# A Fourier filter and an MLP mixer on one core: the first batch's filter loop, rewritten around one product per frequency

## The chip, the cores and the metric

The kernel runs on one core of one Trainium2 chip. The metric is device time in microseconds (us) of that core. The engines are TensorE (PE; its weight loads, PEld, overlap its matmuls), VectorE (DVE), ScalarE (ACT), GpSimd (POOL) and SyncE (SP). SP, ACT and POOL also issue DMAs, each from its own queue in program order. All times of single instructions come from one profiled execution.

## The reference

```python
X = np.fft.rfft(x, axis=1)                        # x: (8, 3008, 256) float32
Y = X * (filt_r + 1j * filt_i)[None]              # filt: (1505, 256)
x = np.fft.irfft(Y, n=3008, axis=1)               # float32
h = np.maximum(x.transpose(0, 2, 1) @ w_tok1, 0.0) @ w_tok2    # (3008, 256), (256, 3008)
u = x + h.transpose(0, 2, 1)
return u + np.maximum(u @ w_ch1, 0.0) @ w_ch2     # (256, 1536), (1536, 256)
```

The four mixer weights arrive as 64-bit floats. Matmuls are float32.

## The kernel before, in words

**The filter.** A length of 3008 is 47 x 64. For each batch, `a_unit` (24 of them; one matmul, `L434`, on a tile of x, then an ACT copy) makes the transform over the 64. For each of the 32 remaining frequencies k, `b_unit(k)` makes the transform over the 47 (matmul `L494` into a PSUM bank), and DVE multiplies by the filter: `p1` is the bank times the real part (`L506`), `p2` the bank's other half times the imaginary part, once with a minus sign (`L507`) and once without (`L508`). Then `bi_unit(k)` multiplies by the inverse table (`L518`). For the first batch it takes p1 and p2 as two accumulating matmuls on the same table; for later groups of two batches DVE adds them first (`L510`). ACT copies the result out (`L524`) and stores it to the scratch tensor g (`L529`), two frequencies a store. Batches go in groups: (0), (1, 2), (3, 4), (5, 6), (7).

**The loads of the loop.** The filter comes in 16 chunks of two frequencies, six DMAs each, into three buffers: chunks 1 and 2 of the first batch on SP, the others on POOL (`filt_load`, `L218` to `L225`). The real part fills the lower 64 partitions, the imaginary part the upper; `filt_double` copies the real part to the upper half on ACT (`L230`). The tables `wb` come on SP (`L454`).

**The weights.** A 64-bit weight tile is loaded to a staging buffer and converted: an ACT copy makes `top` (`L250`); DVE shifts and merges the sign (`L252`, `L253`), masks (`L255`) and computes `rest` (`L257`); top + rest is the float32 value. Twelve W1 tiles and the first `BY_PE` W2 tiles are summed on PE, by two matmuls each (`L289`, `L290`) and an ACT copy (`L292`), the other W2 tiles and the channel weights on DVE (`L278`). There are 12 W1 and 16 W2 tiles, then 2 and 10 of the channel weights. `convert()` ends one tile, starts the ACT copy of the next and issues a load some tiles ahead (`fill`).

**The opening.** Twelve tiles are converted beside the 32 frequencies of the first batch. Then the last parts of g are read back (`t4_load`, `L564`, on SP), the other 16 tiles are converted, and after 18 of the 28 tiles `token_sums(0)` is put into PE's order (96 matmul instructions, `L570`). A Relu on ACT gives h1; `u_unit` (`L600`, `L592`) needs h1 and all of W2 and makes the first 512 columns of u; then the mixer begins.

**The mixer.** For each batch there are 6 blocks of 512 (the last 448) tokens and 6 items in each (jp = 0 to 5). An item has three places. In place 0 come `up_first` (PE `L693`, DVE `up_middle`), one pending DVE step, `h_sums` of the item before (DVE, into t) and `down` part 0 of it (PE `L727`); in place 1 `up_last` (PE `L709`, then DVE and a Relu on ACT, `L714`) and, where due, a step of the next group's filter (an `a_unit`, or `b_unit(k)` with `bi_unit(k-1)`); in place 2 `down` part 1. Parts of the next block's u are made at the places (jp, place) of a map: `u_quarter` has four, with PE matmuls `L614` (and `L592` in parts 2 and 3) into a bank that DVE reads. After the last part the sums `v_steps` (t13, then t2 and t4 together, called t24) are pending DVE steps. All DVE sums have the one line `L671`.

**The banks.** The transforms, `u_quarter` and the token sums share the PSUM banks acc and b:

```python
def free_bank():
    turn.reverse()
    if turn[0] in held:
        turn.reverse()
    return turn[0]
```

`b_unit` of the later groups puts its bank into `held` until `bi_unit` reuses it. Everything is in a hand-written order (`tc.manual_schedule`); an engine runs its instructions in that order and waits for buffers.

Of the kernel before, what the change touches and what calls it, by code (L numbers as in the profile page):

```python
# [46 lines left out]
BY_PE = 6  # L47
# [77 lines left out]
def kernel(  # L125
# [68 lines left out]

    filts = [glob.tile([P, 2, KC, D], FP32, name="filt%d" % i) for i in range(FB)]
# [16 lines left out]
    def filt_load(c, first):  # L212
# [3 lines left out]
        q = nc.gpsimd if first and c not in (1, 2) else nc.sync  # L216
        for src, i, p0 in ((filt_r, 0, 0), (filt_i, 1, HALF)) + (() if first else ((filt_r, 0, HALF),)):
# [10 lines left out]
    def filt_double(c):  # L228
        t = filts[c % FB]
        nc.scalar.copy(out=t[HALF:P, 0], in_=t[0:HALF, 0])  # L230
# [11 lines left out]
    def halves(st, n, pair):  # L242
# [11 lines left out]
                                       op0=ALU.bitwise_and, op1=ALU.bitwise_or)  # L254
        nc.vector.tensor_scalar(out=rest_i, in0=top_i, scalar1=0xFF800000, scalar2=None, op0=ALU.bitwise_and)  # L255
# [12 lines left out]
    def rounded(st, n, parts, late):  # L268
# [6 lines left out]
        yield next(h)  # L275
        top, rest = next(h)
# [7 lines left out]
    def on_chip(stat, top, rest, n, parts):  # L284
# [9 lines left out]
        behind.append((ended[0] - 1, f))  # L294

    def w1_load(i):
# [13 lines left out]
        h = halves(st, 512, spare_pair())  # L310
        yield next(h)
        on_chip(wai_t, *next(h), 512, [(lambda v: v, w1[:, 2 * i:2 * i + 2, :].rearrange("p a t -> p (a t)"))])

    def w2_load(i):
# [15 lines left out]
        if i < BY_PE:  # L330
            h = halves(st, n + more, spare_pair())
            yield next(h)
            on_chip(ident, *next(h), n + more, parts)
        else:
            yield from rounded(st, n + more, parts, False)
# [42 lines left out]
    begin, copy, end = iter(tiles), iter(tiles), iter(tiles)  # L378
# [6 lines left out]
    def sum_up():  # L385
        while behind:
            behind.pop(0)[1]()

    def convert():

        ended[0] += 1
        while behind and behind[0][0] < ended[0] - 2:
            behind.pop(0)[1]()
        advance(end)
        advance(copy)
        fill(6)
# [46 lines left out]
    def dft(bs):  # L443
# [44 lines left out]
        def b_unit(k):  # L488
            tag = ("b", "pg")[k % 2] if first else free_bank()
# [10 lines left out]
            if first:  # L500
                p1, p2 = p1[:, 0:1], p1[:, 1:2]
                prods[k] = (p1, p2)
            else:
                p2 = p2p.tile([P, nb, D], FP32, tag="p2", name="p2")
                prods[k] = (p1,)
# [3 lines left out]
            if not first:  # L509
                nc.vector.tensor_tensor(out=p1, in0=p1, in1=p2, op=ALU.add)  # L510

        def bi_unit(k):


            ps = bank("acc" if first else held.pop(0)).rearrange("p (b d) -> p b d", b=2)[:, 0:nb, :]
            parts = prods.pop(k)
            for i, p in enumerate(parts):
                nc.tensor.matmul(ps[0:KR], wbs[k // WC][:, k % WC, P:], p, start=(i == 0), stop=(i == len(parts) - 1))  # L518
# [18 lines left out]
        if first:  # L537
            filt_double(0)
        for k in range(K2 + 1):
            if k < K2:  # L540
# [10 lines left out]
                if first and k % KC == KC - 1 and k + 1 < K2:  # L551
                    filt_double(k // KC + 1)
            if k >= 1:
                bi_unit(k - 1)
            yield
# [243 lines left out]
    def mix(next_ready):  # L799
# [11 lines left out]
        own = ({(3, 2): 0, (4, 2): 1}, {(2, 2): 0, (3, 2): 1, (4, 0): 2, (4, 2): 3})  # L811
# [69 lines left out]
    with tc.manual_schedule():  # L881
# [4 lines left out]
        rounds = 0  # L886
        second = dft(GROUPS[1])
        for i, _ in enumerate(dft(GROUPS[0])):
# [4 lines left out]
            if i < NXC:  # L893
                if i in (1, 3, 5, 7, 9):
                    start()
                if i == NXC - 1:
                    advance(copy)
                    for t, src in ((wa, wa_d), (wai, wai_d), (ident, ident_d)):
                        nc.scalar.dma_start(t, src)
            elif k >= 0:  # L900
                if (k + 1) * (A // 2) // K2 > k * (A // 2) // K2:
                    convert()
                    rounds += 1
# [3 lines left out]
                elif k == 25:  # L907
                    next(second)
# [9 lines left out]
        for i in range(rounds, A // 2 + TC * N2 // NG):  # L918
            convert()
            if i - rounds < XB:  # L920
                next(second)
            if i == A // 2 + BY_PE - 1:
                sum_up()
                acc = token_sums(0)
# [62 lines left out]
```

## Time and profile before

| | us |
|---|---|
| median of 7 runs | 2573.13 (2568.05 to 2574.78) |
| the profiled execution's own time | 2572.48 |
| its span, first to last instruction | 2570.7 |
| busy PE / DVE / ACT / POOL | 2493.2 / 1944.6 / 660.0 / 575.7 |
| first batch's loop over k (PE) | 30.2 to 108.6 |
| token sums of batch 0 (PE) | 123.2 to 144.0 |
| mixer's first matmul | 156.5 |

A row of the groups reads: line, engine, operation, output<-inputs, shapes and count, then busy us, mean ns of one, then idle us of the engine before them and what ended it. A row of the timeline reads: start, us, engine, line, operation, count, and in brackets the idle time before it and what ended it. PE busy is modelled for pipelined matmuls, so a busy PE is not always at its peak. The granted clock is the TensorE clock as a share of full speed.

### The profile page before, as it was taken

The page shows a single profiled execution, that of the slowest core. Times are in us where ns is not written, and L with a number is a line of the kernel's source. Part 1 is how long each engine was busy: PE and PEld are TensorE (multiplying, and loading weights), DVE is VectorE, ACT ScalarE, POOL GpSimd, SP SyncE. Part 2 cuts the span into 40 slices and gives each one's busy share as a digit, 9 for nine tenths or more (in the row PEclk, how much of TensorE's full clock was granted, in tenths as well). Part 3 has the DMA queues.
Part 4 walks back from the last instruction along what each step waited for, and adds up shares of the span by engine and source line. Part 5 has one row for each costly group of instructions (what it writes and reads, how often), then busy time and mean ns, then how long its engine had stood idle before and what let it go on. Part 6 is the DMA issues. An engine that isn't in the chain of part 4 may idle for free.

```text
span 2570.7 us, 32318 instructions
## 1 busy us (share of the span) xinstructions
PE 2493.2 (97%) x11204; PEld 2054.5 (80%) x11204; DVE 1944.6 (76%) x3668; ACT 660.0 (26%) x1312; POOL 575.7 (22%) x1051
## 2 busy tenths in 40 slices
PE   6989999999999999999999999999999999999998
PEld 3557666888888777898888777898888888898887
DVE  7897888577686998756776889856788587757776
ACT  3533222122221222212221222212222122212222
POOL 4553322211211121122121111221211121211222
PEclk8989999999999999999999999999999999999999
DMA  8864434233332332213332333213333222111100
GB/s 211 232 204 146 129 116 145 94 102 107 111 115 74 99 105 76 93 55 105 116 109 86 90 118 97 88 34 110 99 110 91 66 76 71 40 31 37 44 13 20
DMA packets 166932, 248.39 MB, mean 97 GB/s; under 512 B 35184, under 2 KB 112450, under 8 KB 166768
## 3 DMA queue, kind: packets, MB, share of 16 engines
q1 hardware_dynamic: 94176, 152.20, 19.4%
q0 software_dynamic: 32640, 46.51, 7.2%
q10 hardware_dynamic: 39952, 47.61, 5.8%
q8 instruction: 89, 1.46, 0.2%
q14 instruction: 75, 0.61, 0.1%
HBM read 168.96 MB, written 77.22 MB: 96 GB/s over the span
## 4 chain that ended last, share of the span: by engine, by line
PE 70%; DVE 18%; DMA 2%; issue 2%; ACT 2%; DVEq 0%; ACTq 0%; SPq 0%; POOL 0%; POOLq 0%
PE ps_po L727 24%; PE ps_pg L693 14%; PE ps_pg L709 10%; DVE t L671 4%; DVE hh L671 3%; PE ps_acc L570 3%; PE ps_b L614 2%; PE ps_b L570 2%; PE ps_acc L614 2%; DVE u L671 2%; DVE s L671 2%; PE ps_acc L592 2%; PE ps_b L592 2%; DVE p L508 1%; DVE p L507 1%
## 5 line engine op out<-in xcount | busy, mean ns | idle before, releaser
L772 POOL DMA_DIRECT2D out_dram<-r x757 | 410.4, 550 | 1777.8 <-ACT t L524 741.3
L671 DVE TENSOR_TENSOR hh<-ps_pg,s 128x512 f32<-128x512 f32 (+3 forms) x864 | 483.0, 587 | 281.9 <-ACT s L696 271.7
L714 ACT ACTIVATE hh<-hh 128x512 f32<-128x512 f32 (+1 forms) x576 | 347.9, 621 | 1178.3 <-DVE hh L671 1178.3
L727 PE MATMUL ps_po<-t,wc 128*128 128x256 f32 (+1 forms) x2304 | 537.2, 376 | 6.0 <-DVE t L671 5.0
L727 PEld LDWEIGHTS ps_po<-t,wc 128*128 128x128 f32 x2304 | 436.2, 190 | 130.8 <-issue 55.7
L693 PE MATMUL ps_pg<-v,wc 128*128 128x256 f32 (+1 forms) x1728 | 415.2, 377 | 2.5 <-DVE v L671 2.4
L727 PE MATMUL ps_po<-hh,wc 128*128 128x256 f32 (+1 forms) x1728 | 412.8, 375 | 0.2 <-ACT hh L714 0.2
L693 PEld LDWEIGHTS ps_pg<-v,wc 128*128 128x128 f32 x1728 | 328.1, 191 | 43.7 <-DVE v L671 6.4
L727 PEld LDWEIGHTS ps_po<-hh,wc 128*128 128x128 f32 x1728 | 328.7, 191 | 37.6 <-ACT hh L714 0.5
L709 PE MATMUL ps_pg<-u,wc 128*128 128x256 f32 (+1 forms) x1152 | 294.0, 378 | 4.3 <-DVE hh L671 4.0
L671 DVE TENSOR_TENSOR t<-t,hh 128x256 f32<-128x256 f32 (+1 forms) x576 | 244.8, 425 | 19.8
L709 PEld LDWEIGHTS ps_pg<-u,wc 128*128 128x128 f32 x1152 | 217.0, 190 | 40.1 <-DVE hh L671 13.5
L671 DVE TENSOR_TENSOR s<-ps_pg,hh 128x512 f32<-128x512 f32 (+1 forms) x288 | 196.1, 681 | 31.1 <-PE ps_pg L693 0.9
L671 DVE TENSOR_TENSOR t<-hh 128x512 f32<-128x512 f32 (+1 forms) x288 | 193.0, 670 | 0.6 <-ACT hh L714 0.6
L696 ACT COPY s<-ps_pg 128x256 f32<-128x256 f32 (+1 forms) x288 | 105.8, 367 | 338.7 <-PE ps_pg L693 314.9
L709 PE MATMUL ps_pg<-v,wc 128*128 128x256 f32 (+1 forms) x576 | 169.4, 376 | 0.0
L693 PE MATMUL ps_pg<-u,wc 128*128 128x256 f32 (+1 forms) x576 | 169.3, 376 | 0.0
L671 DVE TENSOR_TENSOR u<-ps_b,u 128x512 f32<-128x512 f32 (+3 forms) x111 | 63.5, 572 | 99.6 <-PE ps_b L614 81.0
L671 DVE TENSOR_TENSOR u<-ps_acc,u 128x512 f32<-128x512 f32 (+3 forms) x99 | 57.4, 580 | 95.4 <-PE ps_acc L614 79.2
L693 PEld LDWEIGHTS ps_pg<-u,wc 128*128 128x128 f32 x576 | 109.4, 190 | 22.6 <-issue 10.9
L709 PEld LDWEIGHTS ps_pg<-v,wc 128*128 128x128 f32 x576 | 109.2, 191 | 13.0
L518 PE MATMUL ps_acc<-p,wb 128*96 128x256 f32 (+1 forms) x256 | 97.5, 482 | 12.7 <-ACT t L524 6.1
(123 smaller groups left out, 2518.5 us busy)
## 6 DMA issues: line engine op xcount, KB each, us to landing
w<-w_tmp SPq DMA_DIRECT2D x35, 896.0 KB
g_tmp<-t ACTq DMA_DIRECT2D x128, 192.0 KB
out_dram<-r POOLq DMA_DIRECT2D x698, 32.0 KB, 1.8
x<-in_x_dram SPq DMA_DIRECT2D x173, 128.0 KB
z_tmp<-t ACTq DMA_DIRECT2D x84, 256.0 KB
t<-z_tmp SPq DMA_DIRECT2D x112, 192.0 KB
t<-g_tmp SPq DMA_DIRECT2D x42, 512.0 KB
wb<-wbi_t SPq DMA_DIRECT2D x80, 224.0 KB
```

The lines of the kernel that those rows point to most:

```text
L507: nc.vector.scalar_tensor_tensor(out=p2[re], in0=ps[im], scalar=-1.0, in1=fi, op0=ALU.mult, op1=ALU.mult)
L518: nc.tensor.matmul(ps[0:KR], wbs[k // WC][:, k % WC, P:], p, start=(i == 0), stop=(i == len(parts) - 1))
L570: nc.tensor.matmul(acc[:, t, :], w1[:, a, ts(t, P)], t4[b, a // TC4][:, a % TC4, :], start=(a == 0 and t == 0), stop=(a == A - 1 and t == ...
L592: nc.tensor.matmul(ps[:, ds(q * P, n)], t4[b, c][:, r, ts(dh, P)], wai[:, 0:n], start=(first and q == 0), stop=(not first and q == 3))
L614: nc.tensor.matmul(ps[:, ds(j * hw, hw)], h1[:, n, :], w2m[m % 2][:, at, 0:hw], start=(i < 2 and j == 0), stop=(j == len(todo) - 1))
L671: nc.vector.tensor_tensor(out=out, in0=in0, in1=in1, op=op)
L693: nc.tensor.matmul(ps[:, 0:hw], chan[0][:, jp, n, :], mov, start=True, stop=True)
L696: nc.scalar.copy(out=s[:, 0], in_=g[0][:, 0, 0:hw])
L709: nc.tensor.matmul(ps[:, 0:hw], chan[0][:, jp, n, :], mov, start=True, stop=True)
L714: nc.scalar.activation(out=hs, in_=hs, func=AF.Relu)
L727: nc.tensor.matmul(po[i][:, j, 0:hw], chan[1][:, jp, n, :], mov, start=(jp == 0 and first == 1), stop=(jp == JP - 1 and last == 1))
L772: q.dma_start(rows[g, e, :, ds(h * A + 4 * m, n)], blocks[ts(g, CW), h, e, 0:n])
```

## The change

For the first batch:

- One DVE operation multiplies the bank, read twice, by both filter parts. Both parts are loaded to the lower partitions and `filt_double` copies both to the upper ones. The sign and the swap of halves go into a second inverse table, `turn_i`, which two ACT operations per chunk make from the first (`table_turn`).
- `b_unit` takes both its banks from the pool pg, and `bi_unit` alternates between acc and b. The doubling and the table turn come after the output copy in ACT's order.
- Chunk 2 of the filter is loaded from POOL.

For the weights: a conversion has a middle and an end as separate half steps; 20 tiles instead of 12 are converted beside the loop; the ACT copies run two tiles ahead; loads run five ahead instead of six; 4 W2 tiles instead of 6 are summed on PE. `token_sums(0)` stands right behind the loop. The second group's first x loads come after the loop, and two of its a_units no longer come before the last W2 tiles.

For the mixer: in batches 1 to 7, parts 1 to 3 of `u_quarter` move to earlier places.

```diff
-BY_PE = 6
+BY_PE = 4
+IN_B = 20
...
-        q = nc.gpsimd if first and c not in (1, 2) else nc.sync
-        for src, i, p0 in ((filt_r, 0, 0), (filt_i, 1, HALF)) + (() if first else ((filt_r, 0, HALF),)):
+        q = nc.gpsimd if first and c != 1 else nc.sync
+        for src, i, p0 in ((filt_r, 0, 0), (filt_i, 1, 0 if first else HALF)) + (() if first else ((filt_r, 0, HALF),)):
...
-        nc.scalar.copy(out=t[HALF:P, 0], in_=t[0:HALF, 0])
+        nc.scalar.copy(out=t[HALF:P], in_=t[0:HALF])
+    turn_i = sp.tile([P, 4, WC, KR], FP32, tag="s", name="turn_i")
+    def table_turn(g, wb):
+        wi, to = wb[:, :, P:], turn_i[:, g % 4]
+        nc.scalar.copy(out=to[0:HALF], in_=wi[HALF:P])
+        nc.scalar.activation(out=to[HALF:P], in_=wi[0:HALF], func=AF.Copy, scale=-1.0)
...
     def convert():
-        ended[0] += 1
-        while behind and behind[0][0] < ended[0] - 2:
-            behind.pop(0)[1]()
+        convert_middle()
+        convert_end()
+    def convert_middle():
+        advance(middle)
+        sum_up()
+    def convert_end():
+        ended[0] += 1
         advance(end)
         advance(copy)
-        fill(6)
+        fill(5)
...
-            tag = ("b", "pg")[k % 2] if first else free_bank()
+            tag = "pg" if first else free_bank()
...
             if first:
-                p1, p2 = p1[:, 0:1], p1[:, 1:2]
-                prods[k] = (p1, p2)
+                nc.vector.tensor_tensor(out=p1, in0=ps.to_broadcast([P, 2, D]), in1=t[:, :, k % KC, :], op=ALU.mult)
+                prods[k] = (p1[:, 0:1], p1[:, 1:2])
+                return
...
-            ps = bank("acc" if first else held.pop(0)).rearrange("p (b d) -> p b d", b=2)[:, 0:nb, :]
+            ps = bank(free_bank() if first else held.pop(0)).rearrange("p (b d) -> p b d", b=2)[:, 0:nb, :]
...
-                nc.tensor.matmul(ps[0:KR], wbs[k // WC][:, k % WC, P:], p, start=(i == 0), stop=(i == len(parts) - 1))
+                wi = turn_i[:, k // WC % 4, k % WC] if i else wbs[k // WC][:, k % WC, P:]
+                nc.tensor.matmul(ps[0:KR], wi, p, start=(i == 0), stop=(i == len(parts) - 1))
...
-                if first and k % KC == KC - 1 and k + 1 < K2:
-                    filt_double(k // KC + 1)
             if k >= 1:
                 bi_unit(k - 1)
+            if first and k % KC == KC - 1 and k + 1 < K2:
+                filt_double(k // KC + 1)
+                table_turn(k // KC + 1, wbs[k // KC + 1])
...
-        own = ({(3, 2): 0, (4, 2): 1}, {(2, 2): 0, (3, 2): 1, (4, 0): 2, (4, 2): 3})
+        own = ({(3, 2): 0, (4, 2): 1}, {(2, 2): 0, (3, 0): 1, (3, 2): 2, (4, 0): 3})
...
-                if (k + 1) * (A // 2) // K2 > k * (A // 2) // K2:
-                    convert()
-                    rounds += 1
+                while half < 2 * IN_B * (k + 1) // K2:
+                    if half % 2:
+                        convert_end()
+                    else:
+                        convert_middle()
+                    half += 1
...
-                elif k == 25:
-                    next(second)
...
-        for i in range(rounds, A // 2 + TC * N2 // NG):
+        next(second)
+        acc = token_sums(0)
+        for _ in range(A // 2 + TC * N2 // NG - IN_B):
             convert()
-            if i - rounds < XB:
-                next(second)
-            if i == A // 2 + BY_PE - 1:
-                sum_up()
-                acc = token_sums(0)
```

## The prediction

> **What bounds the kernel now.** I read the page first. TensorE (PE) is at nine tenths or more in 37 of 40 slices; only the first, third and last are not.
>
> ```profile
> PE 2493.2 (97%) x11204; PEld 2054.5 (80%) x11204; DVE 1944.6 (76%) x3668; ACT 660.0 (26%) x1312; POOL 575.7 (22%) x1051
> PE   6989999999999999999999999999999999999998
> ```
>
> So there are two places to look: the opening 150 us, which the diff rewrites, and the long steady part, where any new PE wait is lost time. For the opening I asked for busy time by stage; columns are stretch, length, busy us of PE, weight load, DVE, ACT, POOL, granted clock, DMA share, GB/s.
>
> ```profile
> 38.20:41.80 3.60, 0.09 (x2) 0.00 (x1) 2.10 (x5) 0.98 (x2) 2.17 (x5) 1.00 0.28 77
> 84.00:108.60 24.60, 23.78 (x85) 14.06 (x84) 23.06 (x50) 11.73 (x25) 12.61 (x23) 1.00 0.82 237
> 108.60:118.00 9.40, 9.34 (x25) 4.19 (x24) 6.76 (x16) 5.93 (x13) 1.61 (x3) 1.00 1.03 215
> 123.20:144.00 20.80, 20.80 (x97) 18.05 (x95) 19.70 (x42) 6.24 (x11) 9.04 (x17) 1.00 0.87 251
> 144.00:148.60 4.60, 1.17 (x3) 0.30 (x2) 4.36 (x11) 1.34 (x3) 2.46 (x5) 0.99 0.66 179
> 148.60:154.70 6.10, 6.10 (x23) 4.11 (x24) 5.55 (x10) 1.17 (x2) 0.07 (x1) 0.73 0.01 3
> ```
>
> The first batch's loop over 32 frequencies runs from 30.2 to 108.6 us, 78.4 us, with DVE at 94% in its settled part. Then 16 weight tiles are left to convert; DVE does them until 148.6. PE runs the token sums (L570) from 123.2 to 144.0, and then waits for the last converted W2 tile:
>
> ```profile
> 142.80 1.24 PE L570 MATMUL ps_b<-t,w 128*128 128x256 f32 x5
> 144.73 1.13 PE L600 MATMUL ps_acc<-w,h 128*128 128x512 f32 x2 [0.69 <-ACT h L582]
> 148.60 2.08 PE L600 MATMUL ps_acc<-w,h 128*128 128x512 f32 x2 [2.75 <-DVE w L278]
> ```
>
> **The loop.** Prices are from its groups of instructions and DMA queues (30 to 112 us):
>
> ```profile
> L524 ACT COPY t<-ps_acc 96x256 f32<-96x256 f32 x32 | 11.8, 367 | 25.9 <-PE ps_acc L518 24.7
> L230 ACT COPY filt<-filt 64x512 f32<-64x512 f32 x14 | 8.6, 616 | 12.2 <-DMA filt<-in_filt_r_dram 6.4 <-DVE both L252 2.1 <-DVE p L506 1.6
> L507 DVE SCALAR_TENSOR_TENSOR p<-ps_b,filt 64x256 f32<-64x256 f32 x16 | 6.8, 426 | 2.1 <-DMA filt<-in_filt_i_dram 1.7
> L253 DVE SCALAR_TENSOR_TENSOR both<-st,both 128x512 uint32<-128x512 uint32 x12 | 8.3, 693 | 0.5
> q1 hardware_dynamic: 4437, 10.18, 50.7%
> q0 software_dynamic: 2976, 4.83, 22.4%
> q10 hardware_dynamic: 3134, 2.96, 12.2%
> ```
>
> DVE before: 32 products of 0.424 + 0.426 + 0.418 us are 40.6; 12 W1 conversions of 0.443 + 0.693 + 0.429 + 0.693 = 2.26 us are 27.1; with 0.025 us between operations 71 us. After: one product of 128x512 from PSUM, priced by the page's s<-ps_pg,hh row at 0.681 us, is 21.8; conversions are 12 of 2.26, four W2 tiles for PE at 1.82 and four summed on DVE at 1.82 + 0.83, 45.0; with gaps 70 us. The 19 us freed are spent on eight more tiles.
>
> PE: 32 x 6 instructions of 0.215 us, 12 W1 sums of 1.72 and four W2 sums of 1.26 make 67 us, against 62. ACT: the doubling copy grows from 512 to 1024 elements. The rows 96x256 (0.367) and 96x512 (0.572) give 0.8 ns an element, so 1.03 us, 15 of them; 30 table turns of 64x192 at 0.32 (the 96x256 row, 0.37, is the upper bound); 32 output copies, 20 rounding copies, 15 copies of sums and 16 DMA issues: 64 us against 41. DMA: the queues were busy 85.3% of 82 us, 70 us. Some six more W2 tiles (0.386 MB, at q0's 3.8 us per MB) add 8.8; the two x tiles that move behind the loop take 2.1 out: 77 us.
>
> So the loop keeps its DVE sum but loses its slack: four resources between 64 and 77 us instead of one at 71. For it: the 3.6 us hole at 38.2 (both PE and DVE waited for filter chunk 2, whose issue on SP stood behind a 7.3 us wait) goes, because chunk 2 is now issued from POOL, idle from 18 to 33 us. The single output bank's 6.1 us of PE waits for the L524 copy go too, but DVE was the later one there, so I give nothing. Against it: in-order engines with little slack wait on each other, and the doubling now needs both filter halves on ACT, ahead of rounding copies. I take a loop 1 us longer, bounds 5 us shorter (hole gone, early half clock shortened) and 9 longer (10% coupling loss on 77 us plus late filters).
>
> The Trainium skill, DMA: Bandwidth & Descriptors, section Issuing engines are not separate DMA queues, speaks against that gain: transfers issued from any engine share the same 16 DMA engines, and spreading them saves only issue time. By that rule alone the loop would be 3.6 us longer than I take it. The row decides: in that hole the DMA share was 0.28, so what lacked was the issue.
>
> **Behind the loop.** PE now goes straight to the token sums. They need the last chunk of g written and read back: before, the loop's last matmul ended at 108.6, its store was issued at 109.1, SP was released for the first last-part load at 115.7, and a load takes some 2 us: token sums could start at 118, not 123.2. Here PE has nothing to hide the 9.5 us (before, W1 and W2 sums did). An idle stretch costs clock: after 3.6 us idle before 148.6 the clock was 0.73 over 6.1 us, 3.4 us of half rate, 1.7 us lost. Sums: 118 + 20.8 + 1.7 = 140.5, Relu 0.7, first L600 at 141.2 with all W2 ready: DVE's eight tiles take 8 x 2.7 = 22 us, to 131. Gain 148.6 - 141.2 = 7.4, and 1.7 more because the 148.6 stretch no longer starts cold: 9.1, less the loop's 1: **8.1 us**. If the loop's queue drains sooner and g lands in 3 us, 3 more; if x loads or weights hold the read-back, 3 less.
>
> Two a_units of the second group lose their place beside the conversions and land among the mixer's: 2 x 0.86 = **1.7 us** back (a place with nothing else late; up to 4 if they wait for x, as the others at 160 to 190 us did).
>
> BY_PE 4 for 6 moves two tiles' sums from PE to DVE, 2 x 0.83 us, covered by the 10 us that DVE is done before the Relu; without that cover 1.7 us. Rounding copies two tiles ahead take the third of the three pairs of buffers (hh, hh, r); nothing else uses them before the mixer. Were one not free, a copy of 0.67 us would wait once a tile, in 20 tiles 13 us of ACT, which only the loop's slack there (78 - 64) hides. fill(5) begins a load when its buffer's last reader is done, so POOL no longer stands before it as it did at 99 to 111 us (12.9 us on L292); no filter load is left behind it there, so nothing is gained.
>
> **The steady part.** The second map of u_quarter places moves part 1 to (3, 0). There its PSUM bank is the one that the filter's next b_unit at (3, 1) takes: free_bank gives the bank not held. So b_unit's matmul waits for the two DVE reads of part 1, 1.15 us, queued behind h_sums:
>
> ```profile
> 1011.05 1.46 PE L727 MATMUL ps_po<-hh,wc 128*128 128x256 f32 x6
> 1012.34 0.68 DVE L671 TENSOR_TENSOR t<-hh 128x512 f32<-128x512 f32 x1
> 1012.35 1.03 PE L709 MATMUL ps_pg<-u,wc 128*128 128x256 f32 x4
> 1013.05 0.89 DVE L671 TENSOR_TENSOR t<-t,hh 128x256 f32<-128x256 f32 x2
> 1013.64 1.02 PE L494 MATMUL ps_acc<-t,wb 96*128 96x512 f32 x2
> 1018.15 1.15 DVE L671 TENSOR_TENSOR u<-ps_b,u 128x512 f32<-128x512 f32 x2 [0.29 <-PE ps_b L614]
> ```
>
> With part 1's 0.86 us of PE ahead of L709, L494 would be due at 1014.50; h_sums end at 1013.94, the bank is free at 1015.1: 0.6 us. I did the same for every such block: 12 have a b_unit there with k over 0, eleven at 0.3 us and this one, 3.9 us. Ten blocks without a filter step get t24 (0.85 us) ahead of h_sums at (5, 0), where t13 (0.68) stood; before, a 0.85 us step ahead of h_sums cost 0.12 us each time: 1.2. Behind L494 on PE stand bi_unit and the down matmuls, all delayed. **5.1 us** lost; bounds 0 (if other waits absorb it) and 7.
>
> **The sum.** -8.1 + 1.7 + 5.1 = -1.3. The profiled execution took 2572.48 us (span 2570.7); 2571.2, and its 0.65 us below the median of 2573.13 added: 2572. A measurement of this kernel can tell some 0.2%, 5.1 us, from no change, so the forecast is no change.
>
> **Rivals.** *Slower: the loop becomes bound by transfers.* Its DMA share was 0.82 to 1.08 outside the hole, and 77 us of transfers in 79 leaves nothing. Filter chunks then land late, ACT's doubling waits, and behind it output and rounding copies. It decides from a loop of 85.8 us on, 7.4 over before; at 88 the sum is 2580. Against: the last five W2 tiles begun are not needed in the loop.
>
> *Faster: the bank wait is absorbed and the hole's gain is whole.* Loop 4 us shorter, steady part +1: -13.1 + 1.7 + 1 = -10.4, 2563.
>
> *It doesn't do what it says:* u_units still wait for W2, because the eight late tiles wait for loads; first L600 at 148, a gain of 0.6 against 1.7 + 5.1: 2579.
>
> **Chances.** No change 0.39 (2568 to 2578 its own range); transfer-bound loop 0.20, late W2 0.10, together slower 0.30; faster 0.31. The range 2561 to 2584 leaves out about two in ten.
>
> **What would show it.** Right: 32 L506-like products of 0.68 us; DVE 66 to 70 us busy in the loop; loop end 105 to 114; token sums starting 8 to 11 us later after an idle, half clock PE; first L600 within 2 us of Relu; 12 new waits of L494 on DVE u. Wrong: filter DMA waits on ACT over 10 us, or no L494 waits at all.

## The result, and the profile after

The changed kernel took 2578.56 us (median of 14 runs, 2573.73 to 2583.99), the kernel before 2572.24 (34 runs, 2568.05 to 2577.19): a ratio of 1.0025 (95% interval 1.0018 to 1.0032). It is 6.3 us slower, past the 5.1 us that the prediction called no change, and inside its range.

The profiled execution is a long one (its own time 2581.64, span 2579.9, 9.2 over the span of before), so the account below adds up to 9.2, of which some 3 are this execution's. The lines move: `L494` is now `L514`, `L506` `L522`, `L518` `L539`, `L524` `L545`, `L529` `L550`, `L564` `L587`, `L570` `L593`, `L600` `L623`, `L614` `L637`, `L671` `L694`, `L218`/`L225` `L220`/`L227`, `L230` `L232`, the W2 load `L321` `L334`. The table turns are `L239` and `L240`.

First the page: PE's busy time and its 40 slices. The steady part is as full as before; the loss is in the first slices.

```profile
PE 2485.6 (96%) x11196; PEld 2052.5 (80%) x11196; DVE 1923.4 (75%) x3606; ACT 677.3 (26%) x1342; POOL 582.2 (23%) x1057
PE   7689999999999999999999999999999999999998
```

Busy time by stage, columns as before the change: stretch, length, busy PE, weight load, DVE, ACT, POOL, granted clock, DMA share, GB/s. The second row is the end of the loop, the next three the idle stretch behind it, then the token sums and the way to the mixer.

```profile
38.00:42.00 4.00, 3.88 (x14) 2.05 (x13) 2.75 (x5) 2.69 (x5) 1.70 (x4) 1.00 1.04 238
100.00:113.00 13.00, 8.27 (x32) 4.95 (x32) 11.83 (x24) 9.01 (x19) 5.98 (x11) 1.00 0.77 229
113.00:118.00 5.00, 0.00 (x0) 0.00 (x0) 4.77 (x12) 1.15 (x3) 1.15 (x2) 0.69 1.02 218
118.00:124.00 6.00, 0.00 (x0) 0.00 (x0) 5.76 (x13) 1.28 (x3) 2.24 (x6) 0.50 1.02 277
124.00:130.40 6.40, 0.00 (x0) 0.02 (x1) 6.16 (x13) 1.23 (x3) 3.25 (x7) 0.50 1.04 172
130.40:153.80 23.40, 23.38 (x96) 19.92 (x96) 7.74 (x16) 1.33 (x2) 4.41 (x8) 0.89 0.47 106
153.80:161.60 7.80, 7.11 (x29) 4.09 (x29) 3.75 (x7) 3.48 (x6) 3.09 (x6) 1.00 0.00 1
```

The hole at 38 us is gone. But the loop ends at 113.0, not 108.6, and the token sums start at 130.4, not 123.2. In between PE does nothing for 17.4 us, and the DMA engines are full. The timeline shows the way: the last store of g is issued at 113.4, SP issues the first last-part read-back when that store has landed, at 123.7, and PE starts at 130.4. The profile names no releaser for PE there; by the updates of the semaphore that the first token sum waits for, the first of the six read-backs had landed on its last DMA engine at 130.32.

```profile
113.42 0.33 ACTq L550 DMA_DIRECT2D g_tmp<-t  x1
...
123.70 0.77 SPq L587 DMA_DIRECT2D t<-g_tmp  x2
...
130.42 1.19 PE L593 MATMUL ps_b<-t,w 128*128 128x256 f32 x2 [17.43 <-issue]
```

Below, "release" is the time from the issue of the last store to the issue of the first last-part read-back (10.3 us here), and "landing" the time from there to the first token sum (6.7 us here).

Where the 9.2 us arise: the mixer's first matmul 161.6 for 156.5 (+5.1); from there to the end of batch 0's items, 371.6 for 370.1 (+1.5); the later batches' items up to the last, 2025.9 for 2023.8 (+2.1); behind that +0.5.

The loop's groups of instructions and DMA queues (30 to 113 us):

```profile
L522 DVE TENSOR_TENSOR p<-ps_pg,filt 128x512 f32<-128x512 f32 x32 | 22.0, 688 | 20.1 <-ACT filt L232 9.8 <-PE ps_pg L514 7.8 <-ACT w L304 1.1
...
L232 ACT COPY filt<-filt 64x1024 f32<-64x1024 f32 x16 | 16.7, 1043 | 8.1 <-DMA filt<-in_filt_i_dram 6.8 <-issue 1.0
...
L239 ACT COPY turn_i<-wb 64x192 f32<-64x192 f32 x16 | 5.6, 350 | 0.4
...
q1 hardware_dynamic: 3849, 9.28, 47.8%
q0 software_dynamic: 3458, 7.15, 30.9%
q10 hardware_dynamic: 3552, 3.15, 14.1%
```

The work is priced right, but DVE is idle 20 us in front of the product, 9.8 of them for the doubled filter (`L232`, which itself waits 6.8 us for filter DMAs) and 7.8 for its bank.

### The profile page after: what moved, and what is told of

Same layout as the page of the kernel before. It is cut to its first block, busy times and chain, and to the rows that moved or that the text cites. A ratio compares the mean times of both kernels' runs of the same rounds, so it can differ in the third digit from the quotient of the medians.

```text
span 2579.9 us, 32269 instructions
## 1 busy us (share of the span) xinstructions
PE 2485.6 (96%) x11196; PEld 2052.5 (80%) x11196; DVE 1923.4 (75%) x3606; ACT 677.3 (26%) x1342; POOL 582.2 (23%) x1057
## 4 chain that ended last, share of the span: by engine, by line
PE 75%; DVE 16%; issue 2%; ACT 2%; DMA 2%; POOL 1%; ACTq 0%; DVEq 0%; SPq 0%; POOLq 0%
PE ps_po L750 25%; PE ps_pg L716 15%; PE ps_pg L732 11%; PE ps_b L593 4%; DVE t L694 3%; DVE hh L694 3%; PE ps_acc L637 2%; PE ps_b L637 2%; PE ps_acc L593 2%; DVE u L694 2%; DVE s L694 2%; PE ps_acc L615 2%; PE ps_b L615 2%; PE ps_acc L454 1%; PE ps_acc L539 1%
## 5 line engine op out<-in xcount | busy, mean ns | idle before, releaser
L694 DVE TENSOR_TENSOR hh<-ps_pg,s 128x512 f32<-128x512 f32 (+3 forms) x864 | 483.0, 587 | 348.3 <-ACT s L719 340.6
L732 PE MATMUL ps_pg<-u,wc 128*128 128x256 f32 (+1 forms) x1152 | 294.2, 378 | 2.9 <-DVE hh L694 2.9
L694 DVE TENSOR_TENSOR t<-t,hh 128x256 f32<-128x256 f32 (+1 forms) x576 | 246.0, 427 | 19.8
L732 PEld LDWEIGHTS ps_pg<-u,wc 128*128 128x128 f32 x1152 | 217.3, 191 | 38.0 <-DVE hh L694 11.5
L694 DVE TENSOR_TENSOR s<-ps_pg,hh 128x512 f32<-128x512 f32 (+1 forms) x288 | 196.1, 681 | 30.4 <-DVE hh L694 0.5
L694 DVE TENSOR_TENSOR t<-hh 128x512 f32<-128x512 f32 (+1 forms) x288 | 193.6, 672 | 0.6 <-ACT hh L737 0.6
L732 PE MATMUL ps_pg<-v,wc 128*128 128x256 f32 (+1 forms) x576 | 168.9, 375 | 0.0
L593 PE MATMUL ps_b<-t,w 128*128 128x256 f32 x480 | 107.2, 386 | 18.5 <-issue 17.4
L732 PEld LDWEIGHTS ps_pg<-v,wc 128*128 128x128 f32 x576 | 109.1, 190 | 13.0
L593 PEld LDWEIGHTS ps_b<-t,w 128*128 128x128 f32 x480 | 92.9, 194 | 32.3 <-issue 17.8
L694 DVE TENSOR_TENSOR u<-ps_acc,u 128x512 f32<-128x512 f32 (+3 forms) x105 | 61.1, 582 | 76.8 <-PE ps_acc L637 60.3
```

Source lines behind the costliest of these rows:

```text
L593: nc.tensor.matmul(acc[:, t, :], w1[:, a, ts(t, P)], t4[b, a // TC4][:, a % TC4, :], start=(a == 0 and t == 0), stop=(a == A - 1 and t == ...
L694: nc.vector.tensor_tensor(out=out, in0=in0, in1=in1, op=op)
L732: nc.tensor.matmul(ps[:, 0:hw], chan[0][:, jp, n, :], mov, start=True, stop=True)
```

## The experiments

Eighteen kernels were run. Unless noted, each is the changed kernel with one edit. Marks from their traces, in us; "gap" is from the loop's last matmul to the first token sum, "mixer" the mixer's first matmul, "steady" from batch 1's first item to the last item. In the expectations, "table tiles" and "the second token table" are W2.

| kernel | loop | its end | gap | mixer | steady | time |
|---|---|---|---|---|---|---|
| before | 78.4 | 108.6 | 14.6 | 156.5 | 2023.8 | 2572.24 |
| after | 82.6 | 113.0 | 17.4 | 161.6 | 2025.9 | 2578.56 |
| e1_own_back | 80.3 | 110.9 | 16.4 | 158.5 | 2024.8 | 2577.48, one run |
| e2_own_alone | 77.4 | 108.9 | 14.6 | 157.9 | 2028.1 | 2579.03, one run |
| e3_light_w2 | 82.6 | 112.8 | 13.2 | 157.5 | 2026.2 | 2577.1, one run |
| e4_w2_behind | 82.7 | 112.9 | 9.5 | 153.9 | 2026.0 | 2574.01, one run |
| e5_four_turns | 81.5 | 112.0 | 12.6 | 155.4 | 2026.2 | 2577.39, one run |
| e6_in_b12 | 74.8 | 105.2 | 13.3 | 184.7 | 2025.9 | 2605.78, one run |
| e8_parts_hold | 81.2 | 112.6 | 5.1 | 149.4 | 2026.0 | 2568.16, one run |
| e9_filt_sp | 92.0 | 122.2 | 8.8 | 161.7 | 2025.9 | 2579.72, one run |
| e10_all | 91.8 | 122.3 | 5.4 | 158.6 | 2024.4 | 2575.12 |
| e12_best | 83.6 | 114.3 | 5.1 | 149.6 | 2025.2 | 2571.14 |
| e14_fb4 | 86.1 | 116.3 | 16.8 | 164.4 | 2026.8 | 2584.61, one run |
| e15_best_fb4 | 86.9 | 116.8 | 4.9 | 153.3 | 2025.8 | 2569.06 |
| e17_by0 | 82.3 | 113.3 | 13.0 | 156.7 | 2026.6 | 2577.48 |
| e18_best_by0 | 81.8 | 112.7 | 5.0 | 148.9 | 2024.5 | 2569.57 |
| e19_best_by0_b16 | 81.9 | 112.2 | 6.3 | 150.3 | 2023.8 | 2569.58 |
| e20_half_filt | 74.8 | 106.1 | 10.3 | 147.0 | 2026.9 | 2571.7, one run |
| e21_w2_sp | 78.8 | 109.1 | 10.1 | 150.8 | 2026.4 | 2571.56 |
| e22_best_w2_sp | 82.5 | 112.8 | 4.9 | 148.2 | 2024.5 | 2565.84 |

An opening scatters from one profiled execution to another: two pairs of kernels have the same opening, and their loops took 82.6 (after) and 80.3 us (e1), and 81.2 (e8) and 83.6 (e12). So a difference of some 3 us between two loops shows nothing by itself. The kernel before took 2570.18 to 2571.74 beside these runs.

### The steady part: e1_own_back, e2_own_alone

e1 puts the four own first steps back to their places of before; e2 is the kernel before with only their new places.

```diff
-        own = ({(3, 2): 0, (4, 2): 1}, {(2, 2): 0, (3, 0): 1, (3, 2): 2, (4, 0): 3})
+        own = ({(3, 2): 0, (4, 2): 1}, {(2, 2): 0, (3, 2): 1, (4, 0): 2, (4, 2): 3})
```

> The changed kernel with the old places of u_quarter. If the bank wait of b_unit on part 1 is what the steady part loses: 251 items from item 36 to item 287 take 2023.8 us as before the change, 2.1 us less than in the changed kernel, and the matmul waits of 0.08 us at L514 in the blocks with a filter step are gone. If the steady part's loss came from the opening (shifted loads): no difference. The prediction's own price of 5.1 us would make it 5 us less.

> The kernel before, with only the new places of the four own first steps of a_unit: one bank each for (3,0), (3,2) and (4,0), so that b_unit's first step at (3,1) comes to a bank that the turn before has just given back. The opening is that of before. Theory 'the bank wait costs what the changed kernel showed': the steady part from the twelfth work item's end to the last's is 2.0 to 2.5 us longer than before's 2023.8, all of it in the blocks that have a filter step, and the opening is as before within its own scatter of 3 us. Rival 'the steady part's 2 us come from the rounding or the opening's offset': the steady part is 2023.5 to 2024.3.

Block by block against before, the changed kernel loses 0.10 to 0.33 us in sixteen blocks, most of them 0.12 or 0.3, *gains* 0.08 in six of those without a filter step, and gains 0.20 and 0.26 in two others. In e1 this pattern is gone (its remaining 1.0 us lies in four single blocks); in e2 it is there, though all else is the kernel before. e2's total of +4.3 is more than expected; 1.7 of it is one block, which no other trace shows and which stays unexplained. Over all traces the steady part has a median of 2026.2 us in the twelve with the new places and 2024.5 in the eight with the old: the places cost some 1.7 us. The waits of `L514` that were forecast are there: twelve, at the twelve blocks, some 0.08 us each and 0.95 in all, too short for the lists of waits; e1 has none of them, and e2 has twelve at the same places.

This is the changed kernel's timeline in the very block that the prediction worked out:

```profile
1017.85 1.46 PE L750 MATMUL ps_po<-hh,wc 128*128 128x256 f32 x6
1018.17 0.69 DVE L694 TENSOR_TENSOR s<-ps_pg,hh 128x512 f32<-128x512 f32 x1
1018.78 0.68 DVE L694 TENSOR_TENSOR t<-hh 128x512 f32<-128x512 f32 x1
1019.14 1.03 PE L637 MATMUL ps_b<-w 128*128 128x256 f32 x4
...
1020.01 1.03 PE L732 MATMUL ps_pg<-u,wc 128*128 128x256 f32 x4
1020.30 1.15 DVE L694 TENSOR_TENSOR u<-ps_b,u 128x512 f32<-128x512 f32 x2
1020.87 0.59 PE L732 MATMUL ps_pg<-v,wc 128*128 128x256 f32 x2
...
1021.55 1.10 PE L514 MATMUL ps_b<-t,wb 96*128 96x512 f32 x2
```

The two reads of ps_b release `L514`, as predicted: in all twelve blocks it starts 0.10 us after the second read's end. But `L514` could not have gone before 1021.46 (1020.87 + 0.59, the end of `L732`), and the bank was free at 1021.45 (1020.30 + 1.15): the wait is 0.08 us, not 0.6. DVE's sums t started 0.93 us after the down matmuls, where before they had started 1.29 after them, and part 1's own 0.86 us on PE used up most of the rest.

### Behind the loop: e4_w2_behind, e3_light_w2, e8_parts_hold

e4 keeps the loads of the weight tiles past the twenty-second (the last six of W2 and the channel weights) back until the last read-backs are issued, and issues those six on SP, behind them.

```diff
+    begun, limit = [0], [22]
-        while begun[0] < len(tiles) and ...
+        while begun[0] < min(len(tiles), limit[0]) and ...
-        nc.gpsimd.dma_start(st[:, 0:n + more], moe_w_tok2...)
+        (nc.sync if i >= 10 else nc.gpsimd).dma_start(st[:, 0:n + more], moe_w_tok2...)
...
             t4_load(0, c, PARTS[2], P)
+        limit[0] = 99
+        fill(5)
```

> The last six W2 tiles are issued from SP behind the read-back of g, nothing left out. Theory Q: 1.2 MB fewer in front of the last store, which is 5 us at 240 GB/s: token sums start 4 to 6 us earlier (125) and the whole is 4 us faster than the changed kernel unless W2 is then late (DVE's last tile after the Relu). Theory E: token sums at 130 as before, and the last W2 tiles later.

The release came after 6.6 us (10.3 in the changed kernel), the landing after 2.4 (6.7), the mixer started 7.7 us earlier. e8 adds to e4 a read-back in three parts, with the middle part's loads in the loop:

```diff
-PARTS = (0, 64, 112)
+PARTS = (0, 64, 96, 112)
+                elif k in (27, 28):
+                    for c in range(3):
+                        t4_load(0, 3 * (k - 27) + c, PARTS[1], PARTS[2])
```

> W2's last six tiles behind the read-back, and the read-back of g in four parts, rows 64 to 96 already at k = 27 and 28. Theory Q: in the run with W2 behind, 1.2 MB of second-part read-back still stood in front of the last store (6.6 us to its reader); two thirds of it now go earlier, so 4 to 5 us, and the mixer starts 1.5 to 3 us earlier than there (152 to 153). If the round trip is fixed at 6.6 us: no change against that run.

The release came after 2.2 us, the landing after 2.5, token sums started 5.1 us after the loop, the mixer 12.2 us earlier than in the changed kernel:

```profile
113.06 0.31 ACTq L550 DMA_DIRECT2D g_tmp<-t  x1
115.25 2.62 SPq L587 DMA_DIRECT2D t<-g_tmp  x6
117.72 0.76 PE L593 MATMUL ps_b<-t,w 128*128 128x256 f32 x1 [5.10 <-issue]
```

The window behind the loop shows what differs; its DMA share is 0.33 where the changed kernel had 1.02:

```profile
113.00:118.00 5.00, 0.28 (x1) 0.31 (x2) 3.33 (x8) 0.03 (x1) 0.00 (x0) 0.50 0.33 92
```

All eight kernels that hold these loads back have gaps of 4.9 to 9.5 us. The changed kernel and e1, e3, e5, e6, e14, e17, e20 and e21, which do not, have 10.1 to 17.4 (e9, whose loop lasts 9 us longer, 8.8). So the traffic in front of the round trip and beside it is what made it long.

e3, meant for the same question, leaves nine of the sixteen W2 loads out:

> Leaves out the loads of nine of the sixteen W2 tiles (their conversions work on the seventh tile's data again). Theory Q, the transfers' queue: the loop ends 3 to 5 us earlier (near 108.5), the last store of g reaches its reader in under 6 us instead of 10.3, the read-back lands in under 4 us instead of 6.7, and the token sums start near 119 instead of 130.4. Theory E, engines waiting on each other and a fixed round trip of store and load: loop end 113, token sums at 130, as in the changed kernel.

It did not decide it: the release took 10.4 us, as in the changed kernel, the landing only 2.4, as in e4. The channel weights' loads, next in the queue, moved up into the gap. Nor did it thin out the loop before 90 us, where the W1 tiles and the first W2 tiles are loaded.

### The loop: what does not hold it

e5 makes only the first four groups' table turns, e6 converts 12 tiles beside the loop instead of 20, e9 issues every second filter chunk on SP, e14 gives the filter a fourth buffer and loads three chunks ahead.

```diff
-                table_turn(k // KC + 1, wbs[k // KC + 1])                       # e5
+                if k // KC < 3:
+                    table_turn(k // KC + 1, wbs[k // KC + 1])
-IN_B = 20                                                                      # e6
+IN_B = 12
-        q = nc.gpsimd if first and c != 1 else nc.sync                          # e9
+        q = nc.gpsimd if first and (c == 2 or c % 2 == 0) else nc.sync
-        t, k0 = filts[c % FB], c * KC                                           # e14
+        t, k0 = filts[c % (FB + first)], c * KC
-                        filt_load(k // KC + 2, first)
+                        filt_load(k // KC + 3, first)
```

> Leaves out the table turns of chunks 4 to 15, twelve times two operations of 0.35 us on ACT, 8.5 us of its 64 in the loop; old turned tables are used instead. Theory E (ACT's in-order work holds the loop): the loop ends 3 to 8 us earlier than 113. Theory Q: ACT was waiting for filters anyway, loop end within 1.5 us of 113.

> Twelve tiles beside the loop instead of twenty, all else as in the changed kernel. Theory Q (weights crowd the loop and the read-back) and theory P (POOL's issue of filter chunks, with W2 loads between them, sets the pace): the loop ends at 104 to 109 instead of 111 to 113, and the read-back of g takes 3 to 6 us less; but 16 tiles of 2 to 2.8 us then stand behind the loop on DVE, 41 us, so the mixer starts at 155 to 160 all the same. If the new steps of the loop themselves (doubling, turning, one product) were to blame: loop end 111 to 113.

> The changed kernel with the odd filter chunks issued from SP, the even ones from POOL. Theory P: POOL's issues of filter chunks follow one another without a gap (4.5 us a chunk) from 60 us on, so with half of them elsewhere the loop ends at 102 to 107 instead of 111 to 113, and the whole is 4 to 8 us faster than the changed kernel. Theory Q: the engines of the transfers are 93% busy, so the loop ends within 2 us of 111 to 113.

> The changed kernel, with a fourth buffer for the filter of the first batch, so that a chunk's two loads are issued three chunks ahead of the products that read it and not two. Nothing else is changed. Theory 'cycle of three filter buffers' (a chunk's loads are issued in some 4.5 us, land 3 to 6 us later, are doubled in 1.0 us, and the buffer is given back only by the chunk's last product, so that three buffers hold the loop to about 4.6 us a chunk): ScalarE's doubling waits under 2 us in all for the filter where it waited 6.8, VectorE's products under 4 us for it where they waited 9.8, and the loop ends at 104 to 109 us where it ended at 113.0; the total is some 3 us under that of the changed kernel, if what lies behind the loop keeps its length. Rival 'the loop is full of transfers' (77 us of full DMA time in 83 us): the loads come earlier but share the same bandwidth, the waits only move, and the loop ends at 111 to 114. Rival 'the order of work on the three engines' (eviction, product and doubling each wait for one another): the waits for the filter go down but the loop ends at 111 to 113.

ACT's turns do not hold the loop (81.5 us). Eight tiles fewer shorten it by 7.8 us, to 3.6 under that of before (and ruin what is behind it, where the last W2 tile was ready at 176.8 us). Chunks on SP stand behind that queue's own waits, 92.0 us. The fourth buffer made it longer, 86.1 us: that theory fell.

### The loop: TensorE or the filter: e17_by0, e20_half_filt

e17 takes TensorE's 16 products for W2 tiles away; e20 leaves out the filter loads of the last ten chunks.

```diff
-BY_PE = 4                                                                      # e17
+BY_PE = 0
-                    if k // KC + 2 < K2 // KC:                                  # e20
+                    if k // KC < 4:
                         filt_load(k // KC + 2, first)
```

> The changed kernel with BY_PE=0: the first four tiles of the second token table are summed by VectorE like the rest, not by two products with the identity matrix each on TensorE and a copy on ScalarE. The tiles, their loads and all else stay. Theory 'TensorE's work sets the loop' (its busy time in the loop was 70.0 us before and 74.8 after, its idle time 8.4 and 7.8; it is busy 29.5 of the first 29.6 us): the 16 products of 0.48 us go, 7.7 us, so TensorE is busy 67 to 69 us in the loop and the loop ends at 104 to 108 us where it ended at 113.0; the mixer starts 3 to 8 us before the 161.6 of the changed kernel, and the total is 2571 to 2576. Rival 'the filter's supply sets the loop' (8.8 us of ScalarE's and VectorE's waits at its end): TensorE's busy time falls, its idle time grows by as much, and the loop ends at 110 to 114.

> The changed kernel with the filter loads of the first batch's last ten chunks left out (chunks 6 to 15 then use what lies in the buffers); doublings, products and all else stay. Theory 'TensorE's work sets the loop': TensorE stays busy some 74 us, VectorE's waits for the filter vanish, but the loop still ends at 106 to 111, since only part of TensorE's 8 us of idle time stands behind the filter. Rival 'the filter's supply sets the loop': it ends at 98 to 104.

The whole loop in one row each (columns as above), first the changed kernel:

```profile
30.40:113.00 82.60, 74.81 (x256) 46.46 (x256) 60.91 (x114) 59.03 (x115) 50.76 (x92) 0.94 0.93 237
```

then e17:

```profile
31.00:113.30 82.30, 69.20 (x240) 42.80 (x240) 63.49 (x118) 55.11 (x110) 52.03 (x92) 0.94 0.93 239
```

and e20:

```profile
31.30:106.10 74.80, 71.07 (x256) 45.19 (x256) 60.59 (x114) 58.71 (x115) 17.98 (x32) 0.98 0.87 237
```

e17 took 5.6 us off TensorE and the loop kept its length: idle time took their place. So TensorE, the theory that I held by then, is not the bound. e20 shortened the loop by 7.8 us; the end at 106.1 is on the early edge of the 106 to 111 of the theory of TensorE, and past its rival's 98 to 104. TensorE is then busy 95%, so little more is to be had from the filter alone. The late filter costs some 5.5 to 8.8 us, measured against the 80.3 to 83.6 of the four loops above. e20 takes the bytes of these loads away with their lateness, so it does not tell the two apart.

### Why the filter is late: e21_w2_sp

POOL's timeline in the kernel before, at the last two chunks (a chunk's loads begin with `L218`): they are issued at 89.2 and 93.5 us, and W2 loads follow.

```profile
88.17 0.56 POOL L321 DMA_DIRECT2D st<-in_moe_w_tok_dram  x1
89.19 0.54 POOL L218 DMA_DIRECT2D filt<-in_filt_r_dram  x1 [0.46 <-DVE p L508]
...
93.47 0.53 POOL L218 DMA_DIRECT2D filt<-in_filt_r_dram  x1 [1.04 <-DVE p L506]
...
96.88 1.64 POOL L321 DMA_DIRECT2D st<-in_moe_w_tok_dram  x3
```

In the changed kernel the last two (now `L220`) stand behind W2 loads that wait for a staging buffer, and come at 94.4 and 102.4:

```profile
91.22 0.56 POOL L334 DMA_DIRECT2D st<-in_moe_w_tok_dram  x1
93.82 0.55 POOL L334 DMA_DIRECT2D st<-in_moe_w_tok_dram  x1 [2.03 <-ACT turn_i L240]
94.37 0.53 POOL L220 DMA_DIRECT2D filt<-in_filt_r_dram  x1
...
101.03 0.56 POOL L334 DMA_DIRECT2D st<-in_moe_w_tok_dram  x1 [1.86 <-DVE both L262]
102.44 0.55 POOL L220 DMA_DIRECT2D filt<-in_filt_r_dram  x1 [0.85 <-ACT w L304]
```

e21 issues all W2 loads on SP:

```diff
-        nc.gpsimd.dma_start(st[:, 0:n + more], moe_w_tok2...)
+        nc.sync.dma_start(st[:, 0:n + more], moe_w_tok2...)
```

> The changed kernel with all loads of the second token table issued on SyncE's queue, so that POOL's queue holds nothing but the filter's loads (and three halves of others) until the loop's end. Bytes, buffers and work stay. Theory 'the filter's loads stand behind table loads that wait for staging buffers': the last chunk's loads are issued at 92 to 97 us where the first of them was issued at 102.4, VectorE's and ScalarE's waits for the filter fall below 8 us in all where they were 16.6, and the loop ends at 104 to 109 where it ended at 113.0. Behind the loop the read-back may come later, since the table loads now stand in front of it on SyncE; the total is open between 2568 and 2580. Rival 'the filter is late by its bytes' (full DMA for 77 of 83 us): the same bytes, so the loop ends at 111 to 115.

Its last two chunks:

```profile
87.94 0.54 POOL L220 DMA_DIRECT2D filt<-in_filt_r_dram  x1 [0.57 <-ACT t L545]
...
93.50 0.54 POOL L220 DMA_DIRECT2D filt<-in_filt_r_dram  x1 [1.47 <-DVE both L268]
```

The loop is 78.8 us long, ending at the late edge of the theory's 104 to 109, with the same bytes and a DMA share that rose from 0.93 to 0.96. That is 3.8 us under the changed kernel, but only 1.5 under e1, which has the changed kernel's opening. The waits that were to fall below 8 us fell only from 16.6 to 12.0. Behind the loop the window from 113 to 118 us has a DMA share of 0.65, the release comes after 7.4 us and the landing takes 2.3, since SP now issues what is left of the W2 loads after the read-backs. This one word brings the time to that of before, 0.9998 (0.9988 to 1.0007).

The Trainium skill, DMA: Bandwidth & Descriptors, section Issuing engines are not separate DMA queues, has it that spreading transfers over issuing engines saves issue time and no bandwidth. The bytes of e21 stayed, but its time fell by 7 us, so here the choice of the engine changed more than issue time: in the changed kernel POOL stands 7.3 us in the loop in front of `L334`, and what is behind it in the queue waits too. How much of the 7 us comes from that, and how much from the shorter gap, no run separates.

### Together

e12 is e8 with the old places; e18 is e12 with BY_PE = 0, e19 that with IN_B = 16; e15 is e12 with the fourth filter buffer; e10 is e12 with every second chunk on SP; e22 is e12 with all W2 loads on SP.

> The changed kernel with two edits: the four own first steps back in the places of before, and the traffic behind the loop lightened (the output read back in three parts, not two, the middle part's six loads issued three rows earlier in the loop; the table tiles past the twenty-second held back till the last read-backs are issued; from the tenth on issued on SyncE). Theory 'the opening lost its gain to the traffic in front of the last store and read-back, and the steady part to the bank wait': the mixer starts at 149 to 153 us where the changed kernel's started at 161.6 and that of before at 156.5, the steady part is 2024 us, and the total is 2564 to 2569, some 4 to 8 us under before. Rival 'the loop's end and start scatter by 3 us and that run was a lucky one': 2568 to 2573, no difference from before.

> The last kernel with the fourth filter buffer of the first one of this set. If three filter buffers hold the loop: the loop ends 4 to 8 us earlier and the total is 2559 to 2565. If the loop is full of transfers or held by the order of work: the same as the last kernel within 2 us.

> The changed kernel with three repairs: own first steps back in their old places, read-back in three parts with the late table traffic held back (both as in e12_best), and BY_PE=0. By the theory of TensorE: the loop ends at 105 to 109, token sums start at 111 to 114 unless the table tiles are late, the mixer starts at 143 to 149, and the total is 2561 to 2567. By the theory of the filter's supply: as e12_best, 2567 to 2573.

> The last kernel with 16 table tiles beside the loop and not 20; the four go behind it, beside the token sums, on VectorE alone. By the theory of TensorE: the loop is as long as in the last kernel within 1 us (VectorE's tiles do not weigh on it), and the total is the same within 2 us. By a theory that VectorE's tiles weigh on the loop too (0.9 to 1.6 us of VectorE a tile): the loop ends 2 to 5 us earlier, and the total is up to 3 us lower.

> e12_best (own first steps in their old places, read-back in three parts, table tiles past the twenty-second held back) with all loads of the second token table on SyncE. By the theory of the queue: loop end 105 to 110, mixer 144 to 150, total 2561 to 2567. By the theory of bytes, or if SyncE's waits only move the delay to the step matrices and the read-back: 2567 to 2574, as e12_best.

Ratios to before: e10 1.0009 (1.0000 to 1.0019), e12 0.9995 (0.9986 to 1.0004), e15 0.9991 (0.9982 to 1.0000), e18 0.9993 (0.9984 to 1.0002), e19 0.9989 (0.9980 to 0.9998), e22 **0.9976** (0.9966 to 0.9985). e10, expected at 2560 to 2564 or at 2567 to 2570, took 2575.1: its loop took 91.8 us, as that of e9. e12, e15, e18 and e19 repair the gap (5 to 6 us) and the places and stop within 0.2% of before; e12, e15 and e18 are above what the theories that they tested gave; e22 beats it by 5.6 us, and its median is 12.7 us below that of the changed kernel. Its loop is where I was wrong again: the last chunk's first load went out at 96.1, but the five others took POOL until 102.9, stopped by waits for earlier filter loads to land (the longest 2.4 us), and the loop took 82.5, 1.1 under that of e12. So W2 on SP is worth 0.2 to 0.3% in both pairs (after and e21, e12 and e22), clear of the noise; that it is so because of the order of POOL's queue in the loop is argued from the rows above and not shown, since only one of the two loops became clearly shorter. How much of the late filter is the full DMA engines themselves, no run separates either.

## Why the prediction was wrong, step by step

The forecast was 1.3 us less; the profiled execution took 9.2 more. Of the difference, 9.8 us arose behind the loop and 3.2 in it, and 3.0 went the other way in the steady part. That the median still lies in the range is partly luck: two errors of opposite sign.

**Loop, +1 us predicted, +4.2 measured.** The prices held: products 0.688 us (0.681), doubling 1.04 (1.03), turns 0.35 and 0.36 (0.32 to 0.37), PE 4.8 us more (5), transfers 0.93 x 82.6 = 77 us (77), the hole gone. DVE's busy time fell from 66.4 to 60.9, more than the 71 to 70 of the sum, so the saving on DVE was real. The step that failed is "The 19 us freed are spent on eight more tiles", with 1 us for the loop in all. e6 has the rewritten steps with twelve tiles, and its loop takes 74.8 us, less than before; with twenty it takes 80.3 to 83.6. With twenty and without the filter's last ten loads (e20) it takes 74.8 again, which suggests that the tiles cost time by making the filter late. Why they do stays open between two causes. One is the step on `fill(5)`, "POOL no longer stands before it" and "no filter load is left behind it there, so nothing is gained", which was read from the kernel before and kept for the changed one: with 20 tiles beside the loop 13 W2 loads are issued by POOL between 30 and 113 us instead of 7, POOL waits 7.3 us in front of them (put down to ACT and DVE, which read the staging buffers), and filter chunks stand behind. The other is the prediction's rival of the transfer-bound loop. Its 77 us of transfers were there, 0.93 of the loop (0.96 in e6 and e21, whose loops are shorter), and it gave a time close to the one measured; but it was to decide from a loop of 85.8 us on, and the loop took 82.6 with a quiet stretch (share 0.77) at its end. "ACT filter-DMA waits over 10 us" as the sign of being wrong was not reached either (6.8): the waits stood on DVE, one step further.

**Behind the loop, 9.1 us gained predicted, 0.7 lost measured** (the mixer starts 48.6 us after the loop's end, 47.9 before). This is the main failure. The step that failed is "SP was released at 115.7, and a load takes some 2 us: token sums could start at 118". It took a release of 6.6 us and a landing of 2 as fixed. The first is read from the kernel before; the second is not. There the first of these loads had landed on its last DMA engine, by the semaphore's updates, at 120.58, 4.9 us after its issue (the row's 4.82 us are the issuing of all six):

```profile
115.70 4.82 SPq L564 DMA_DIRECT2D t<-g_tmp  x6
```

In the changed kernel the same two took 10.3 and 6.7 us, 8 more than predicted, with loads of W2, of the second part of g and of the channel weights in the engines at a share above 1.0. e4 takes part of that traffic away and gets 6.6 and 2.4 us, e8 gets 2.2 and 2.5, and with them token sums at 117.7, where the prediction had put them. "If x loads or weights hold the read-back, 3 less" named the risk at a third of its size. The rest of the step was right: first `L623` 0.7 us after the token sums, all W2 ready by 135.5 (131), PE at half clock after the idle stretch. That cost 2.6 us in the token sums (23.4 for 20.8), against 1.7.

**a_units, 1.7 us predicted, 1.5 measured.** Right. Batch 0's first block scatters by up to 3 us, but its other five together take 1.7 us longer in the changed kernel, and 1.2 to 2.7 in the seventeen others with its order; in e2, where the a_units keep their places, they take the time of before.

**Steady part, 5.1 us predicted, 2.1 measured, about 1.7 of it the places.** Sign, place and mechanism right, size wrong twice: the wait was 0.08 us in the block that was worked out, where 0.6 was predicted, the blocks grew by 0.12 as often as by 0.3, and of the ten without a filter step, which were to lose 0.12 each, six gained 0.08, two lost 0.2 and two stayed. The first came from keeping DVE's start as it was in the block before while moving PE's by 0.86; the second from a price taken from another pair of steps.

Two readings of the prediction were slightly off, and nothing hangs on them: before the loop's hole the DMA share was 0.78 from 30 to 38.2 us, under the 0.82 named as the lowest, and PE was idle 3.4 us, not 3.6, before 148.6.

## What to carry to other kernels

Work that is moved takes its loads along: list for each queue what will now stand in front of the loads that the critical loop needs, and whether that can wait. A round trip through DRAM (store, release, read back) is priced by the traffic in the engines at that moment, so let the bulk wait until the read-back is issued. In the queue that feeds a tight loop, look for loads that wait for a buffer of other work: taking them out gained 5 to 7 us here in two pairs of kernels, though the runs do not show in which stage.

## What the runs showed of the hardware that was not expected

- From the issue of the last store (192 KB) to the release of its reader it took 2.2 us where the engines then had a share of 0.33 (e8), 7.4 at 0.65 (e21), 6.6 at 1.03 (before) and 10.3 at 1.02 (the changed kernel): traffic sets it, but not by the share alone. The first of the six read-backs of 64 KB behind it landed in 2.3 to 2.5 us in e4, e8 and e21, and in 6.7 in the changed kernel.
- After 17.4 us without a matmul the granted clock was 0.50, and 0.89 on average over the next 23.4 us. A gap of 5.1 us (e8) cost as much: 23.9 us for the token sums that took 20.8 without one. In the eighteen kernels with a gap, of 4.9 to 17.4 us, the token sums took 22.5 to 24.0 us, and the clock's price did not grow with the gap's length. The mean of 0.89 over 23.4 us is 5.1 us at half rate, 2.6 lost. The Trainium skill, TensorE: Matmul & The Clock Gate, section What's actually happening, has at least one busy window of some 3.4 us before full rate returns, an estimate of 1.7 to 3.4 us lost as the window falls. The 2.6 us agree; the least of the eighteen, e12's 22.5 us at a mean clock of 0.93, lost 1.5, a little under it.
- POOL stopped between two loads of one filter chunk for up to 2.4 us, until an earlier filter load had landed, while it had nothing else to wait for in the trace. What stops it was not tried.
